# Kernel rows loaded as they lie and folded from channel-major columns, with a copy turned backwards, in a gated mix of two state-space layers

## The chip, the cores and the metric

One core of one Trainium2 chip runs the whole program. The metric is device time in microseconds (us), from the start of one execution to its end; less is better. In a profile the engines are called PE (TensorE matmuls; PEld is its weight load), DVE (VectorE), ACT (ScalarE), POOL (GpSimd) and SP (SyncE, which issues most transfers). Times inside a profile count from the start of its span.

## What is computed

The output is a gated sum of two layers over a sequence of S = 2048 positions and D = 1024 channels, all in bf16:

```python
g = sigmoid((x * gate_w).sum(-1, keepdims=True))
a = S5(x)      # complex diagonal recurrence over t, with B, C matrices of 1024 x 1024
b = H3(x, k, v)
return g * a + (1 - g) * b

# H3, for each channel d:
k_shift[t] = sum over i < 4 of k[t - i] * shift_k[i]
kv = k_shift * v
y = irfft(rfft(kv, 2S) * rfft(ssm_k, 2S))[:S]     # a causal convolution of length 2048
return x * (y + kv * ssm_D)
```

ssm_k holds one row of 2048 taps for each channel: shape (1024, 2048), the channel outermost.

## The kernel before

The H3 layer works through eight chunks of 128 channels (NC = 8). The sequence is cut into four blocks of 512 positions (TB), and the transform of a block is a matmul with tables of cosines and sines. As those are even and odd, a block of 512 is first folded: its upper 256 positions plus and minus its lower 256 mirrored about the middle. For the convolution kernel this fold is `fold_K(c)` (lines 471 to 484). It takes the tile kn, which holds positions on the partitions (128) and [16 blocks of 128 positions, 128 channels] beside them. Two matmuls of 512 columns for each of sum and difference and each half mt of the fold, one with the identity `ident` as weights and one with `refl` (the identity with its columns turned, with sign +1 or -1), build the sum in PSUM; a matmul with one row adds ssm_D at position 0. ACT copies the PSUM tile foldk to the tile eok. The last chunk uses `mirror_K` instead.

So kn must have positions on its partitions, while ssm_k lies in memory with the channel outermost: `load("kn", c)` (lines 184 to 191) issues a transposing transfer, `load_t`, on SP.

After the fold, `fwd_K` does the forward transform (PSUM tiles psk, copied by ACT to Kh or into BT); `taps` makes k_shift from kT, the transposed k; `times_v` multiplies by v, mirrors (PSUM tile mirror, ACT copy lo, DVE difference ev); `fwd_V` gives Vh; `products` are DVE's complex products into G; `inverse` gives psz and cv, which goes to memory. Parts of the S5 layer (`Bu`: PSUM tiles odd and even, ACT copies U) are put between.

The order on each engine is written out by hand: every instruction that goes through `put` is tied behind the one before it on its engine (lines 92 to 95), so that calls in the text stand on the engine in that order. Work is written as generators that `step` and `run` move on. PSUM has four tiles in rotation (`psum`, line 81): a new tile waits until ACT or DVE has read the tile that had its buffer before. The tag ld has three buffers for kT, kn, kB and v.

The start (lines 1025 to 1067) is written out too: taps for chunk 0 and DVE's products with v, tables SF, CF and NCF, `columns` (parameter columns), `state_params` (small DVE operations abv, thn, nthn, then th and so on), `inverse_cols` and `inverse_angles` (the rows for the inverse table), the fold of chunk 0, its transforms and products. Then the loop over c from 0 to 6 (lines 1079 to 1199) works at three chunks at a time: products of chunk c, forward transforms of n = c + 1, and fold, taps and v of nn = c + 2, and issues the loads of c + 3. In the loop, ACT's order around the fold of chunk nn is: copies cv, lo, cv, then `dgs(nn)`, then the four evictions of psk of chunk n, then the evictions of foldk.

The first transfers: SP issues the two halves of kT for chunk 0, then kn for chunk 0; ACT's queue takes the shift taps (skr), the first half of v (`load_v0(0)`, line 165), three rows of parameters (line 167), then after a table load the second half of v, ssm_D and gate_w. Transfers that use the hardware queues take one of eight completion semaphores in turn, and a transfer waits until the one before it on its semaphore has landed.

Of the kernel before, what the change touches and what calls it, by code (L numbers as in the profile page):

```python
# [9 lines left out]
ALU = mybir.AluOpType  # L10
ACT = mybir.ActivationFunctionType
BF16 = mybir.dt.bfloat16
# [8 lines left out]
def kernel(  # L21
# [38 lines left out]
    TB = 512  # L60
# [25 lines left out]
    def ps2(shape, name):  # L86
        return psum.tile(shape, F32, name=name, tag="ps")
# [9 lines left out]
    def mm(o, l, r, first, last):  # L97
        put("pe", nc.tensor.matmul, o, lhsT=l, rhs=r, start=first, stop=last)
# [9 lines left out]
    def ts(o, a, s1, s2, op0, op1=None):  # L108
        if op1 is None:
            put("dve", V.tensor_scalar, out=o, in0=a, scalar1=s1, scalar2=None, op0=op0)  # L110
        else:
            put("dve", V.tensor_scalar, out=o, in0=a, scalar1=s1, scalar2=s2, op0=op0, op1=op1)

    def copy(o, a):
        put("dve", V.tensor_copy, o, a)

    def act(o, i, **kw):
        put("act", nc.scalar.activation, out=o, in_=i, **kw)

    def load_t(o, i):  # L120
        put("sp", nc.sync.dma_start_transpose, out=o, in_=i)

    def move(o, i):
        put("sp", nc.sync.dma_start, out=o, in_=i)
# [36 lines left out]
    def load_v0(h):  # L161
        ns = slice(h * NT // 2, (h + 1) * NT // 2)
        nc.scalar.dma_start(out=v0[:, ns], in_=vf.rearrange("(n p) d -> p n d", p=128)[:, ns, 0:128])

    load_v0(0)
    for i, ap in enumerate((A_log_dt, A_Lambda_re, A_Lambda_im)):
        nc.scalar.dma_start(out=prow[i * ND:(i + 1) * ND, :], in_=ap.rearrange("(j p) -> j p", p=128))
    pih = consts.tile([128, 1], F32, name="pih")
    put("dve", nc.vector.memset, pih, math.pi / 2.0)
    magic = consts.tile([128, 1], F32, name="magic")  # L170
# [10 lines left out]
    def hold(column):  # L181
        act(column, pih, func=ACT.Copy)

    def load(which, c, held=False):
        cc = slice(c * 128, (c + 1) * 128)
        if which == "kn":

            t = ld.tile([128, NT, 128], BF16, name="kn", tag="ld")
            if held:
                hold(t[:, 0, 0:1])  # L190
            load_t(t, B_ssm_k[cc, :])
        elif which == "v":

            w = 2 if c == 2 else 1
            if c == NC - 1:
                t = ld.tile([128, NT, 128], BF16, name="v", tag="ld")
            elif c == 2:
                lds["v2"] = xt_pool.tile([128, NT, 2, 128], BF16, name="v2", tag="xT")
            if c < 2:
                t = ld.tile([128, NT, 128], BF16, name="v", tag="ld")  # L200
            elif c < NC - 1:
                t = lds["v2"][:, :, c % 2:c % 2 + w].rearrange("p n k d -> p n (k d)")
            if held:
                hold(t[:, 0, 0:1])
            move(t, vf.rearrange("(n p) d -> p n d", p=128)[:, :, c * 128:(c + w) * 128])
            for k in range(w):
                lds["v", c + k] = t[:, :, k * 128:(k + 1) * 128]
            return
        else:

            t = ld.tile([128, PAD + S], BF16, name="kT", tag="ld")
            put("pool", nc.gpsimd.memset, t[:, 0:PAD], 0.0)
            if held:
                hold(t[:, PAD:PAD + 1])
            load_t(t[:, PAD:], kf[:, cc])
            if c >= 3:
                lds["kB", c] = ld.tile([128, PAD + S], BF16, name="kB", tag="ld")
        lds[which, c] = t
# [35 lines left out]
    def iota_i32(shape, pattern, base, mult, name):  # L254
        ti = u4(shape, I32, name + "_i")
        nc.gpsimd.iota(ti, pattern=pattern, base=base, channel_multiplier=mult)
        return ti

    def iota_f32(shape, pattern, base, mult, name, home=None):
        ti = iota_i32(shape, pattern, base, mult, name)  # L260
        t = u4(shape, F32, name) if home is None else home.tile(shape, F32, name=name)
        copy(t, ti)
        return t

    def flat(ap):
        return ap.rearrange("p a b -> p (a b)")
# [20 lines left out]
    SI = tab_pool.tile([128, 2, 512], BF16, name="SI")  # L287
    colm_i = iota_i32([128, 2], [[256, 2]], 1, 2, "colm")
    fr_i = iota_i32([128, 512], [[4, 512]], 1, 0, "fr_")
    ident = consts.tile([128, 128], BF16, name="ident")  # L290
    make_identity(nc, ident)
    raised = ps2([128, 2, 512], "raised")

# [7 lines left out]
    nc.gpsimd.memset(refl, 0.0)  # L301
    for k, v in enumerate((1.0, -1.0)):
        nc.gpsimd.affine_select(out=refl[:, k], in_=refl[:, k], pattern=[[1, 128]], base=-127, channel_multiplier=1,
                                compare_op=ALU.not_equal, fill=v)
    colm = consts.tile([128, 2], F32, name="colm")
    ts(colm, colm_i, 1.0 / 4096.0, None, ALU.mult)
# [52 lines left out]
    inv = {}  # L359

    def inverse_cols():
        colf = iota_f32([128, 2], [[512, 2]], 1, 4, "colf", home=consts)
        inv["col"] = consts.tile([128, 2], F32, name="colneg")
        inv["at0"] = consts.tile([128, 2], F32, name="colat0")
        ts(inv["col"], colf, -1.0 / 2048.0, None, ALU.mult)
        ts(inv["at0"], colf, 511.0 / 2048.0, None, ALU.mult)

    def inverse_angles():

# [9 lines left out]
    def inverse_table():  # L379

        yield from sincos(flat(inv["room"]), 1024, flat(SI), flat(CI), -TWO_PI)
# [89 lines left out]
    def fold_K(c):  # L471

        kb = lds.pop(("kn", c)).rearrange("p (a f) d -> p a f d", f=4)
        eo = eos["k", c] = eo_pool.tile([128, 2, 2, 4, 128], BF16, name="eok")
        for mt in range(2):
            ps = ps2([128, 2, 4, 128], "foldk")
            for e in range(2):
                mm(ps[:, e], ident, kb[:, :, 2 + mt], True, False)
                mm(ps[:, e], refl[:, e], kb[:, :, 1 - mt], False, mt == 0)
                if mt == 1:  # L480

                    mm(ps[:, e, 0], refl[0:1, e], sD[:, c * 128:(c + 1) * 128], False, True)
            act(eo[:, :, mt], ps, func=ACT.Copy)
            yield

    def mirror_K(c):
# [131 lines left out]
    def fwd_V(c, fis=range(NFI)):  # L618
        eo = eos["v", c]
        if c not in VH:  # L620
            VH[c] = spectrum("V", c)
        for fi in fis:
            fsl = slice(fi * 128, (fi + 1) * 128)
            ps = ps2([128, 2, 4, 128], "psv")
            for cc in range(2):
                tab = CF if cc == 0 else SF
                for mt in range(2):
                    mm(ps[:, cc], tab[:, mt, fsl], eo[cc][:, mt], mt == 0, mt == 1)
            act(of_tile(VH[c], fi), ps, func=ACT.Copy, scale=2.0 / 1024.0)
# [384 lines left out]
    def step(gen):  # L1014
        next(gen, None)

    def run(gen):
        for _ in gen:
            pass
# [5 lines left out]
    none = iter(())  # L1025
    first = first_times_v(0, dg0)
    step(first)
    act(flat(SF), rqf, func=ACT.Sin, scale=TWO_PI)
    put("dve", V.scalar_tensor_tensor, out=flat(hf), in0=rqf, scalar=-1.0, in1=rqf, op0=ALU.mult, op1=ALU.max)
    act(flat(CF), flat(hf), func=ACT.Sin, bias=pih, scale=-TWO_PI)  # L1030
    columns = columns()
    step(columns)
    trow[0] = tab_pool.tile([128, TB], mybir.dt.float16, name="row")
    copy(trow[0], flat(iota_i32([128, 2, HB], [[1, 2], [2, HB]], 0, 0, "row")))
    sp = state_params()
    step(sp)
    step(first)
    inverse_cols()
    ts(NCF, CF, -1.0, None, ALU.mult)
    step(first)  # L1040
    angles = inverse_angles()
    turns = inverse_table()
    run(columns)
    run(fold_K(0))
    step(sp)
    step(angles)
    run(first)
    dg1 = dgs(1, True)
    run(angles)
# [2 lines left out]
    load("kn", 1)  # L1052
    fwd_K(0, (0, 1))
    fwd_V(0, (0, 1))
    step(turns)
    taps(1, dg1)
    step(sp)
# [21 lines left out]
    for c in range(NC - 1):  # L1079
# [47 lines left out]
        step(tabs)  # L1127
        run(back)
        run(old)
        if nn < NC:  # L1130
            dg = dgs(nn)
        if c == 2:
            step(parts)
        fwd_K(n, (0, 1))
# [6 lines left out]
            run(sp)  # L1141
            gate(0)
        step(prod)
        fk = none
        if nn < NC:
            fk = fold_K(nn) if c < 5 else mirror_K(nn)
            step(fk)
            if c < 5:
                step(fk)
            if c == 4:  # L1150
                step(parts)
            if c == 1:
                load_BT(1, 0, True)
            elif c < 5:
                load("v", nn, True)
            step(parts)
            taps(nn, dg)
            if c == 5:
                load("v", nn)
                load_xT(2, held=True)  # L1160
            if nn + 1 < NC:
                load("kT", nn + 1, True)
                load("kn", nn + 1)
                apart = spread(nn + 1)
                step(apart)
                if c == 1:
                    load_BT(1, 1)
                elif c in (2, 3):
                    load_xT(1, (3 - c,))
                run(apart)  # L1170
# [297 lines left out]
```

## Time and profile before

| what | us |
|---|---|
| median of 3 runs | 388.48 (388.27 to 388.70) |
| the profiled execution | 385.94 |
| its span, from first to last instruction | 384.2 |
| PE busy in the span | 373.1 |
| DVE busy in the span | 371.7 |
| ACT busy in the span | 294.3 |

The granted clock of TensorE was 0.999 of full speed. Busy times are of one profiled execution. A matmul of 512 columns is listed with some 380 ns, but such matmuls start 215 ns apart: they are pipelined, and the spacing of their starts, not their listed length, is what a row of them costs. The DMA engines are busy in nearly every slice of the span; 45.6 MB of the 70.7 MB moved go over the queue of SP and its transposing loads.

| stage | from | to |
|---|---|---|
| start, to the first product of chunk 0 on DVE | 0 | 19.4 |
| rest of chunk 0's products | 19.4 | 47.2 |
| chunk loop c = 1 to 5, five products of 23 to 24 us each | 47.2 | 164.8 |
| last chunks, then the S5 layer and the output | 164.8 | 384.2 |

### The profile page before, as it was taken

The numbers are of one execution on the slowest core, as the hardware profiler recorded it, in microseconds if no ns is written. First come the engines' busy times: TensorE is split into PE (matmuls) and PEld (weight loads), VectorE is DVE, ScalarE is ACT, GpSimd is POOL, SyncE is SP. The second block draws the span as 40 slices with busy tenths as digits, with TensorE's granted clock in tenths as the row PEclk, the third lists the DMA queues.
The fourth block names the chain that finished last, engine by engine and source line by source line (L and its number), as shares of the span: only waits on it lengthen the run. The fifth ranks groups of instructions, "written<-read, shape, count | busy, mean of one in ns | idle before, by whom it ended". The sixth has DMA issues, their size and how long they took to land.

```text
span 384.2 us, 6583 instructions
## 1 busy us (share of the span) xinstructions
PE 373.1 (97%) x2411; PEld 196.2 (51%) x2445; DVE 371.7 (97%) x602; ACT 294.3 (77%) x448; POOL 77.1 (20%) x101
## 2 busy tenths in 40 slices
PE   7999899999999999999999999999999999999995
PEld 4556347565484756754454444444444444444442
DVE  8899999999999999999999999999999999999996
ACT  5799997988979789774678799775988869937601
POOL 3011030110301102030002300413414323635000
PEclk9999999999999999999999999999999999999999
DMA  8969999999999997957696999896899999898903
GB/s 166 166 131 226 183 221 213 224 202 146 230 201 221 212 189 162 198 136 136 115 208 142 204 258 203 199 196 122 157 224 184 222 247 236 139 258 153 225 2 109
DMA packets 135506, 70.72 MB, mean 184 GB/s; under 512 B 114921, under 2 KB 117745, under 8 KB 135474
## 3 DMA queue, kind: packets, MB, share of 16 engines
q1 hardware_dynamic: 120912, 45.64, 55.4%
q0 software_dynamic: 12400, 24.12, 36.8%
q10 hardware_dynamic: 2162, 0.54, 0.8%
q8 instruction: 19, 0.31, 0.3%
q14 instruction: 13, 0.11, 0.1%
HBM read 12.86 MB, written 8.39 MB: 55 GB/s over the span
## 4 chain that ended last, share of the span: by engine, by line
PE 75%; DVE 14%; ACT 4%; issue 3%; DMA 3%; SPq 1%; DVEq 0%
PE psy L94 29%; PE both L94 17%; PE psk L94 7%; DVE BT L94 5%; PE psz L94 5%; PE taps L94 4%; DVE wkh L94 4%; PE even L94 3%; PE psv L94 3%; PE foldk L94 3%; PE odd L94 3%; DVE G L94 2%; ACT Vh L94 1%; DMA BT<-in_A_B_im_dram 1%; DMA kT<-in_B_k_dram 1%
## 5 line engine op out<-in xcount | busy, mean ns | idle before, releaser
L94 PEld LDWEIGHTS <-BT 128*128 128x128 bf16 x640 | 61.7, 98 | 49.0 <-DMA BT<-in_A_B_im_dram 0.9
L94 PE MATMUL both<-xT,BT 128*128 128x512 bf16 x375 | 83.4, 379 | 0.9 <-DMA BT<-in_A_B_im_dram 0.4
L94 POOL DMA_DIRECT2D U<-Q x22 | 23.3, 1071 | 90.2 <-ACT Q L94 55.3
L94 PEld LDWEIGHTS <-hb 128*128 128x128 bf16 x256 | 24.9, 98 | 30.2 <-issue 0.3
L94 PEld LDWEIGHTS <-U 128*128 128x128 bf16 x240 | 23.5, 98 | 28.3
L94 PE MATMUL psy<-CT,hb 128*128 128x512 bf16 x156 | 36.6, 379 | 0.2
L94 ACT ACTIVATE Vh<-psv 128x1024 bf16<-128x1024 f32 x32 | 30.8, 1033 | 7.7 <-PE psv L94 7.6
L94 ACT ACTIVATE U<-both 128x512 bf16<-128x512 f32 x44 | 24.2, 594 | 16.0 <-PE both L94 15.5
L94 PE MATMUL psy<-CT,U 128*128 128x512 bf16 x149 | 34.3, 379 | 0.1
L94 DVE TENSOR_TENSOR_SCAN W<-rv,init,A 128x256 bf16<-128x256 f32 x48 | 32.2, 732 | 0.0
L94 POOL DMA_DIRECT2D G<-wkh x8 | 9.7, 1218 | 101.7 <-DVE wkh L94 101.7
L94 ACT ACTIVATE Q<-U,lam 128x512 bf16<-128x512 bf16 (+1 forms) x44 | 25.4, 607 | 3.9 <-DMA CT<-Q 3.9
L94 PE MATMUL psk<-eok,SF 128*128 128x512 bf16 (+1 forms) x119 | 27.9, 354 | 0.3
L94 PEld LDWEIGHTS <-SF 128*128 128x128 bf16 x184 | 18.0, 98 | 19.6 <-issue 1.1
L94 PE MATMUL psz<-G,CI 128*128 128x512 bf16 x64 | 24.3, 380 | 1.4 <-DVE G L94 1.3
L94 PE MATMUL psz<-G,SI 128*128 128x512 bf16 x64 | 24.3, 379 | 0.0
L94 PE MATMUL psy<-CTa,hb 128*128 128x512 bf16 x95 | 22.6, 379 | 0.1
L94 PE MATMUL taps<-dg,kT 128*128 128x128 bf16 (+1 forms) x352 | 21.3, 207 | 1.3 <-DMA kT<-in_B_k_dram 1.3
L94 PEld LDWEIGHTS <-kT 128*128 128x128 bf16 x352 | 20.6, 98 | 2.8 <-DMA kT<-in_B_k_dram 2.2
L94 DVE TENSOR_TENSOR wkh<-BT,Vh 128x3072 bf16<-128x3072 bf16 (+4 forms) x20 | 21.8, 1112 | 0.0
L94 DVE TENSOR_TENSOR wkh<-Kh,Vh 128x3072 bf16<-128x3072 bf16 (+2 forms) x16 | 21.3, 1351 | 0.0
L94 PE MATMUL psy<-CTa,U 128*128 128x512 bf16 x87 | 20.4, 379 | 0.1
(221 smaller groups left out, 838.9 us busy)
## 6 DMA issues: line engine op xcount, KB each, us to landing
U<-Q POOLq DMA_DIRECT2D x22, 256.0 KB, 5.1
G<-wkh POOLq DMA_DIRECT2D x6, 768.0 KB, 8.3
cv_scr<-cv SPq DMA_DIRECT2D x16, 256.0 KB, 3.8
v<-in_B_v_dram SPq DMA_DIRECT2D x5, 512.0 KB, 5.8
out_dram<-m SPq DMA_DIRECT2D x8, 256.0 KB, 6.3
BT<-cv_scr SPq DMA_DIRECT2D x7, 256.0 KB, 7.1
out_dram<-BT SPq DMA_DIRECT2D x7, 256.0 KB, 3.8
ks<-lo POOLq DMA_DIRECT2D x6, 256.0 KB, 7.7
```

What stands on the lines that cost most here:

```text
L94: i = f(*a, **kw)
```

## The change

For chunks 0, 3, 4, 5 and 6 (`by_channel`) kn is loaded with a plain transfer, a channel's row of 4096 bytes to one partition. The new `fold_columns` folds it: first a copy `back` (tile lo) takes the lower 256 positions of each block in reverse order, on DVE for chunk 0 and on ACT for the others; then, for each half mt and each of the four blocks, 128 columns of kn serve as weights against [identity, identity] and 128 columns of back as weights against [identity, -identity], 256 columns each, so that the transposition happens on PE and sum and difference come out side by side. The evictions of foldk to eok are as many and as large as before, with the axes of the PSUM tile in another order.

The reversed copy is put in the loop behind `dgs(nn)` and ahead of the evictions of psk; the matmuls stay where the fold was. For chunk 0 the copy stands on DVE ahead of the first product with v.

Around it: the first half of v is issued behind the three parameter rows on ACT's queue, which also gives it and them other completion semaphores, and kn of chunk 0 shares one with the first parameter row instead of v. The casts of row and colf and its two scalings go from DVE to ACT, ahead of SF; the angle rows come ahead of the fold's evictions on ACT; `state_params` begins after the fold, so that its table load on ACT and its first three DVE operations come later. POOL makes two more 128x128 identities, one of them negative.

```diff
-    load_v0(0)
     for i, ap in enumerate((A_log_dt, A_Lambda_re, A_Lambda_im)):
         nc.scalar.dma_start(out=prow[i * ND:(i + 1) * ND, :], in_=ap.rearrange("(j p) -> j p", p=128))
+    load_v0(0)
...
+    def by_channel(c):
+        return c == 0 or 3 <= c < NC - 1
...
         if which == "kn":
-            t = ld.tile([128, NT, 128], BF16, name="kn", tag="ld")
-            if held:
-                hold(t[:, 0, 0:1])
-            load_t(t, B_ssm_k[cc, :])
+            if by_channel(c):
+                t = ld.tile([128, S], BF16, name="kn", tag="ld")
+                move(t, B_ssm_k[cc, :])
+            else:
+                t = ld.tile([128, NT, 128], BF16, name="kn", tag="ld")
+                load_t(t, B_ssm_k[cc, :])
...
-    ident = consts.tile([128, 128], BF16, name="ident")
+    idents = consts.tile([128, 3, 128], BF16, name="ident")
+    ident = idents[:, 0]
...
+    nc.gpsimd.memset(idents[:, 1:], 0.0)
+    for k, v in ((1, 1.0), (2, -1.0)):
+        nc.gpsimd.affine_select(out=idents[:, k], in_=idents[:, k], pattern=[[1, 128]], base=0, channel_multiplier=-1,
                                 compare_op=ALU.not_equal, fill=v)
...
     def inverse_cols():
-        colf = iota_f32([128, 2], [[512, 2]], 1, 4, "colf", home=consts)
+        colf = iota_i32([128, 2], [[512, 2]], 1, 4, "colf")
         inv["col"] = consts.tile([128, 2], F32, name="colneg")
         inv["at0"] = consts.tile([128, 2], F32, name="colat0")
-        ts(inv["col"], colf, -1.0 / 2048.0, None, ALU.mult)
-        ts(inv["at0"], colf, 511.0 / 2048.0, None, ALU.mult)
+        act(inv["col"], colf, func=ACT.Copy, scale=-1.0 / 2048.0)
+        act(inv["at0"], colf, func=ACT.Copy, scale=511.0 / 2048.0)
...
+    def fold_columns(c):
+        kn = lds.pop(("kn", c)).rearrange("p (a t) -> p a t", t=TB)
+        back = eo_pool.tile([128, 4, 2, 128], BF16, name="lo", bufs=2)
+        rev = back.rearrange("p a f d -> p a (f d)"), kn[:, :, 255::-1]
+        if c == 0:
+            copy(*rev)
+        else:
+            act(*rev, func=ACT.Copy)
+        yield
+        eo = eos["k", c] = eo_pool.tile([128, 2, 2, 4, 128], BF16, name="eok")
+        for mt in range(2):
+            ps = ps2([128, 4, 2, 128], "foldk")
+            for a in range(4):
+                withD = mt == 1 and a == 0
+                mm(ps[:, a], kn[:, a, 256 + mt * 128:384 + mt * 128], idents[:, 0:2], True, False)
+                mm(ps[:, a], back[:, a, mt], idents[:, 1:3], False, not withD)
+                for e in range(2 if withD else 0):
+                    mm(ps[:, a, e], refl[0:1, e], sD[:, c * 128:(c + 1) * 128], False, e == 1)
+            act(eo[:, :, mt], ps.rearrange("p a e d -> p e a d"), func=ACT.Copy)
+            yield
...
     step(first)
+    trow[0] = tab_pool.tile([128, TB], mybir.dt.float16, name="row")
+    act(trow[0], flat(iota_i32([128, 2, HB], [[1, 2], [2, HB]], 0, 0, "row")), func=ACT.Copy)
+    inverse_cols()
     act(flat(SF), rqf, func=ACT.Sin, scale=TWO_PI)
...
     step(columns)
-    trow[0] = tab_pool.tile([128, TB], mybir.dt.float16, name="row")
-    copy(trow[0], flat(iota_i32([128, 2, HB], [[1, 2], [2, HB]], 0, 0, "row")))
-    sp = state_params()
-    step(sp)
+    fk = fold_columns(0)
+    step(fk)
     step(first)
-    inverse_cols()
     ts(NCF, CF, -1.0, None, ALU.mult)
     step(first)
     angles = inverse_angles()
     turns = inverse_table()
+    step(angles)
     run(columns)
-    run(fold_K(0))
+    run(fk)
+    sp = state_params()
     step(sp)
-    step(angles)
     run(first)
...
     fwd_V(0, (0, 1))
+    step(sp)
     step(turns)
...
+        fk = none
         if nn < NC:
             dg = dgs(nn)
+            if by_channel(nn):
+                fk = fold_columns(nn)
+                step(fk)
...
-        fk = none
         if nn < NC:
-            fk = fold_K(nn) if c < 5 else mirror_K(nn)
+            if not by_channel(nn):
+                fk = mirror_K(nn)
             step(fk)
```

## The prediction, made before the changed kernel was run

> **What bounds the kernel now.** I read the page first, then the chain of waits in order of time, then the timeline of the start, the DMA packets of the start by stretch, and last DVE, ACT and PE beside each other in the chunk loop. The page's busy line:
>
> ```profile
> PE 373.1 (97%) x2411; PEld 196.2 (51%) x2445; DVE 371.7 (97%) x602; ACT 294.3 (77%) x448; POOL 77.1 (20%) x101
> ```
>
> Two engines are full at once, so a gain must shorten both, or fall where one of them stands idle. The chain of waits (start, length, what) says where that is:
>
> ```profile
> 0.75 4.90 DMA kT<-in_B_k_dram
> 5.69 1.96 PE taps L94 x32
> ...
> 10.10 2.27 PE foldk L94 x10
> ...
> 12.39 1.03 ACT eok L94
> ...
> 56.36 2.15 PE foldk L94 x10
> ```
>
> The start hangs on a transfer, then on PE and ACT through the fold of chunk 0; from 46 to 137 us the chain runs almost wholly on PE. The timeline of the start:
>
> ```profile
> 0.75 2.59 SPq L94 DMA_TRANSPOSE kT<-in_B_k_dram  x2
> 1.34 0.43 ACTq L163 DMA_DIRECT2D v<-in_B_v_dram  x1
> 5.54 2.09 SPq L94 DMA_TRANSPOSE kn<-in_B_ssm_k_dram  x1
> 6.01 1.22 DVE L94 SCALAR_TENSOR_TENSOR h<-rq 128x1024 f32<-128x1024 f32 x1
> 9.71 0.42 DVE L94 TENSOR_SCALAR NCF<-CF 128x1024 bf16<-128x1024 bf16 x1
> 12.93 1.22 DVE L94 TENSOR_TENSOR ev<-ks,mirror 128x1024 bf16<-128x1024 bf16 x1 [1.03 <-PE foldk L94]
> 19.36 1.23 DVE L94 TENSOR_TENSOR G<-BT,Vh 128x2048 bf16<-128x2048 bf16 x1 [0.75 <-ACT Vh L94]
> ```
>
> kn is issued 2.2 us after SP is free (3.34): in the built program it waits for v's first load, with which it shares a completion semaphore, and 1.34 plus that load's 4.2 us to landing is 5.54. The DMA packets in the stretch 3.25 to 4.5 us (q10 is ACT's queue, q1 SP's):
>
> ```profile
> q10 hardware_dynamic: 1046, 0.26, 112.3%
> q1 hardware_dynamic: 130, 0.03, 16.2%
> ```
>
> The stretch before has 933 packets of q1 alone, the one after 1040 of q1. So v's first half (256 KB, 1024 packets) runs between the two halves of kT, and kT's first half, moved by about 3.5, lands only at 5.65. In the loop, DVE's first product of three chunks waits for Vh:
>
> ```profile
> 94.54 2.29 DVE L94 TENSOR_TENSOR G<-Kh,Vh 128x4096 bf16<-128x4096 bf16 x1 [0.21 <-ACT Vh L94]
> 117.82 2.29 DVE L94 TENSOR_TENSOR G<-BT,Vh 128x4096 bf16<-128x4096 bf16 x1 [0.17 <-ACT Vh L94]
> 141.28 2.29 DVE L94 TENSOR_TENSOR G<-Kh,Vh 128x4096 bf16<-128x4096 bf16 x1 [0.36 <-ACT Vh L94]
> ```
>
> These 0.74 us are all that DVE can win there. ACT and PE in the chunk c = 3:
>
> ```profile
> 100.33 1.09 ACT L94 ACTIVATE dg<-ident,pcol 128x64 bf16<-128x64 bf16 x4
> 101.28 3.79 ACT L94 ACTIVATE BT<-psk 128x1024 bf16<-128x1024 f32 x4
> ...
> 103.23 0.38 PE L94 MATMUL foldk<-kn,ident 128*128 128x512 bf16 x1
> ...
> 105.48 1.92 PE L94 MATMUL odd<-xT,BT 128*128 128x256 bf16 x16
> ```
>
> **The start, step by step.** v's first load moves behind three parameter loads on ACT's queue (0.50, 0.32 and 0.58 us): issued at about 2.8 instead of 1.34. kT's halves then follow each other undisturbed. The transposed kn, alone on the engines, was complete 0.3 to 0.5 us after its last packets (until 9.25 to 9.5, landed 9.74); kT's first half, last packets at 3.5, lands so at 4.0, or with the 1.2 us of a v load still in between at 5.2; I take 4.6, and taps begins 1.1 us earlier. PE then needs, as before, 10.10 - 5.69 = 4.4 us to the fold: 9.0. Fold 2.05 (below), eviction 1.05, then 5.9 from there to Vh (13.42 to 19.33 before): 18.0 instead of 19.33.
>
> DVE does not start earlier: its table arithmetic ends at 7.23 in both. From there: pcol 0.1; the new reversed copy, L; product 1.22; NCF 0.36; product 1.22; three small copies 0.3; PE's mirror 0.25; then 5.7 to G's start as before (12.93 to 18.61, its own readiness) and 0.45 for abv, thn and nthn, which move from before ev to here. That is 16.8 + L for G. Gone from DVE: the row cast (0.42), colf and its two scalings (0.34). ACT takes these (0.6 and 0.3) before SF, which slips from 6.0 to about 6.4; NCF, the first reader of CF on DVE, comes over 1 us later, so nothing. POOL's new memset (0.6) and two selects (0.36 each) push the row iota from 3.29 to 4.6, inside the same cover. ACT's table load (1.28) and dtv move from 8.43 to behind eok, where ACT before did rv and the two angle rows (1.7): 0.1 at most, since the first psk needs PE 1.2 us anyway.
>
> L is unknown: nearest rows are NCF, the same shape forwards (0.42), and the PSUM product of 1024 (1.22). I take 0.6, nearer the former because the types and places are its own. The new wait: the copy needs kn, and DVE's two products, ev and through mirror PE stand behind it. kn, now waiting only for the first parameter row, is issued at about 3.4, needs SP about 0.5 (v's plain loads) instead of 2.09, and carries 0.52 MB, which the transposed load moved in 2.3 us. The engines are taken by kT until 4.8 and by v's two halves for 1.25 us each. kn lands between 7.4 (ahead of v) and 9.7 (behind both); I take 8.2. G starts at 8.2 + 9.5 + 0.6 = 18.3, against PE's 18.0: 1.0 us gained. Ends: 16.8 + 0.42 gives way to PE's 18.0 (1.3 gained); 9.7 + 9.5 + 1.22 = 20.4 (1.0 lost).
>
> The Trainium skill, VectorE: DVE Perf Modes, What auto-detection actually checks, lets a 16-bit copy keep its fast mode at a step of +1 or -1. By that rule L is 0.42 and G starts at 18.1; no run here shows a negative step.
>
> **The loop, chunks 3 to 6.** PE: a fold took 105.48 - 103.23 = 2.25 us: eight matmuls of 512 columns 0.215 apart, and two one-row matmuls that cost 0.25 each. Now 16 of 256 columns: odd, 16 pairs of weights and 256 columns, goes from 105.48 to 107.23, 1.75 us. The one-row pair stands together: 0.3. So 2.05, 0.2 less, four times: 0.8 gained. Below: 0 if the one-row pair costs 0.5.
>
> ACT: one more pass of 128x1024 bf16 per chunk, behind dg and ahead of the psk evictions; row: eok<-kn, 1.06 us, the next starting 0.94 later. Behind it stand four evictions that free PSUM for PE. c = 1: the first is then over at 54.9, the fold that takes its buffer starts at 56.2: covered by 1.3. c = 2: 79.5 against psk at 80.06: covered by 0.5. c = 3: 101.28 + 0.94 + 1.02 = 103.24 against 103.23: 0.1 with the semaphore. c = 4: 126.54 against even at 126.51: 0.1. ACT then catches up in its idle 1.49 us before Vh. If the reversed pass is longer, every tenth over 0.94 costs PE twice, over 1.5 three times.
>
> Plain loads save SP about 2 us a chunk and 0.5 to 1 us of the DMA engines; kn is read a chunk later (issued 67.73, read at 77.5), so that is worth nothing, and costs nothing while loads stay a chunk ahead. PE gains 0.8 - 0.2 = 0.6; DVE could take 0.74. I take 0.5. Past 141 DVE sets the end up to 189.8, and the rest follows it: nothing else changes.
>
> **Sum.** 1.0 + 0.5 - 0.1 = 1.4 us. The profiled execution took 385.94 (span 384.2 and 1.7 around it) and would take 384.5. The median of the runs shown, 388.48, is 2.5 above that execution; with the same difference: 387.1. What a measurement of this kernel can tell from no change is about 0.2%, 0.8 us.
>
> **Rivals.** (1) kn lands behind v's second half, near 9.3: DVE waits for it, G starts at 19.4, the start gains nothing and 0.5 - 0.1 stays: 388.1. For it: both v halves are issued before kn, and the trace shows whole loads running one after the other. Against: they stand on another queue, and kT's two halves ran on either side of one. Chance 0.2.
> (2) Slower: the reversed read is slow on ACT, a place in the loop without cover. Where the next pass starts 2.0 us later instead of 0.94, PE waits 0.5, 1.1 and 1.1 in c = 2, 3, 4; less 0.8 of the folds that is 1.9 late, less 0.9 at the start: 388.5 + 1.0 = 389.5. It decides from about 1.9 on. No row has a reversed operand; the forward ones are all near 1.06. Chance 0.12.
> (3) The twofold number of weight loads shows. Eight more at the 98 ns of a LDWEIGHTS row make a fold 2.05 + 0.8 = 2.85 us, 0.6 over 2.25; four are 2.4 late, and with 0.2 of ACT and 0.9 gained at the start that is 388.5 + 1.7 = 390.2. Against it stand odd's 16 pairs in 1.75 us, weights included. Chance 0.03.
> The Trainium skill, TensorE: Matmul & The Clock Gate, The mechanism, says that weight loads overlap running matmuls only in other row groups, which would make (3) true; odd's pairs, all of full height, disagree.
> (4) The change does what it says but kT lands no earlier, since v's load was not in its way: start 0.3, loop 0.5, less 0.1: 387.8; it is in (1)'s neighbourhood, chance 0.05, faster or same by a hair.
>
> The forecast has 0.6, its own range 386.4 to 387.7. Faster: 0.6 and a little of (4), 0.62. Same: 0.22. Slower: (2), (3) and the late, slow copy of the start, 0.16. The range leaves out (3), half of (2) and a gain over 2.5: 386.0 to 389.3.
>
> **What would show it.** Right: kT's wait ending near 4.6, kn issued near 3.4, G at 18.0 to 18.6, folds of 2.05 us, the three Vh waits nearly gone, ACT's lo<-kn near 1.06. Wrong: DVE idle in front of its lo<-kn until past 9; lo<-kn near 1.2 on DVE or 2 on ACT; PE waiting for psk evictions in c = 3 and 4; fold matmuls more than 0.12 apart.

## The result and the profile after

The changed kernel took 386.12 us (median of 16 runs), the kernel before 388.06 (16 runs, 385.85 to 389.05); the ratio is 0.9955, 95% interval 0.994 to 0.9969, so 1.2 to 2.3 us less. Forecast were 387.1 and a range of 386.0 to 389.3: sign and size hold, though the time lies only 0.1 above the lower bound and below the narrower range, 386.4 to 387.7, to which the forecast gave 0.6. The way to them does not hold, as the profile shows.

One execution of the changed kernel among the 16 was disturbed (2238 us) and is left out of the ratio; the profile after is therefore that of the first experiment, the same kernel run again (384.5 us span, 386.24 with what lies around it). Its busy line, to be set beside the one of before:

```profile
PE 373.7 (97%) x2451; PEld 201.0 (52%) x2485; DVE 371.5 (97%) x599; ACT 298.3 (78%) x455; POOL 77.3 (20%) x104
```

Nothing got shorter here, and the span is 0.3 us **longer** than that of the kernel before (384.2). The chain of waits, start and one fold of the loop (start, length, what):

```profile
5.75 4.57 DMA rows<-in_gate_w_dram
10.32 0.05 issue
10.37 0.51 PE p L94 x8
10.88 2.26 PE foldk L94 x18
...
13.16 1.03 ACT eok L94
```

Before, the start hung on kT until 5.65 and then on PE. Now it hangs on the gate's row, a load of 2 KB that the prediction did not count, and kT is off the chain. The timeline of the start (SP's and ACT's issues, PE, DVE):

```profile
0.74 2.60 SPq L94 DMA_TRANSPOSE kT<-in_B_k_dram  x2
2.66 0.44 ACTq L163 DMA_DIRECT2D v<-in_B_v_dram  x1
3.84 0.37 SPq L94 DMA_DIRECT2D kn<-in_B_ssm_k_dram  x1
4.34 3.14 PE L94 MATMUL taps<-dg,kT 128*128 128x128 bf16 x32
7.94 1.96 PE L94 MATMUL taps<-dg,kT 128*128 128x128 bf16 x32 [0.34 <-DMA kT<-in_B_k_dram]
10.14 0.43 DVE L94 COPY lo<-kn 128x1024 bf16<-128x1024 bf16 x1 [2.28 <-DMA kn<-in_B_ssm_k_dram]
20.75 1.17 DVE L94 TENSOR_TENSOR G<-BT,Vh 128x2048 bf16<-128x2048 bf16 x1
```

taps starts at 4.34 instead of 5.69 and without a wait; then 32 matmuls take 3.14 us, where before they took 1.96. DVE waits for kn until 10.14, and G starts at 20.75, 1.4 us later than in the profile before. Why kn is so late stands in the DMA packets of the stretch 6 to 7 us, when it has been under way for over 2 us (q10 is ACT's queue with v, q1 SP's with kn):

```profile
q10 hardware_dynamic: 875, 0.22, 134.0%
q1 hardware_dynamic: 32, 0.00, 2.4%
```

In the loop, PE's fold and DVE's first products:

```profile
103.96 0.27 PE L94 MATMUL foldk<-ident,kn 128*128 128x256 bf16 x1
...
106.02 1.91 PE L94 MATMUL odd<-xT,BT 128*128 128x256 bf16 x16
```

```profile
95.00 2.28 DVE L94 TENSOR_TENSOR G<-Kh,Vh 128x4096 bf16<-128x4096 bf16 x1
...
118.33 2.29 DVE L94 TENSOR_TENSOR G<-BT,Vh 128x4096 bf16<-128x4096 bf16 x1 [0.23 <-ACT Vh L94]
...
141.69 2.29 DVE L94 TENSOR_TENSOR G<-Kh,Vh 128x4096 bf16<-128x4096 bf16 x1 [0.26 <-ACT Vh L94]
```

A fold takes 106.02 - 103.96 = 2.06 us (2.25 before). Of the three waits for Vh one is gone, two stay (0.23 and 0.26, before 0.17 and 0.36).

How can a kernel whose profile is 0.3 us longer be 1.7 us faster by the medians of the first experiment? Because the profile before is not of the usual run. The first set of runs beside the experiments has 35 of the kernel before: nine from 385.7 to 386.1 and 26 from 387.1 to 388.8, with nothing between; with the two later sets it is 14 of 84 up to 386.45, with a median of 385.8, and 70 from 387.03 to 389.19, with a median of 387.9. The profile before (385.94) is of the small group. The changed kernel's 12 runs beside them lie in one group, 385.34 to 386.35. So what the change does is to take away the large group.

### The profile page after: what moved, and what is told of

Read it like the earlier page. It is cut to its first block, busy times and chain, and to the rows that moved or that the text cites. A ratio compares the mean times of both kernels' runs of the same rounds, so it can differ in the third digit from the quotient of the medians.

```text
span 2236.4 us, 6704 instructions
## 1 busy us (share of the span) xinstructions
PE 2231.0 (100%) x2485; PEld 696.5 (31%) x2485; DVE 374.3 (17%) x599; ACT 310.1 (14%) x455; POOL 76.5 (3%) x104
## 4 chain that ended last, share of the span: by engine, by line
PE 100%; DVE 0%; DVEq 0%; issue 0%
PE psy L94 30%; PE both L94 23%; PE psk L94 13%; PE psv L94 8%; PE psz L94 8%; PE taps L94 5%; PE even L94 5%; PE odd L94 4%; PE foldk L94 4%; PE mirror L94 1%; PE p L94 1%; PE raised L94 0%; DVE BT L94 0%; DVEq L1502 0%; DVE wkh L94 0%
## 5 line engine op out<-in xcount | busy, mean ns | idle before, releaser
L94 PE MATMUL both<-xT,BT 128*128 128x512 bf16 x384 | 508.8, 1705 | 0.0
L94 PEld LDWEIGHTS <-BT 128*128 128x128 bf16 x640 | 204.1, 320 | 464.3 <-issue 464.1
L94 PE MATMUL psy<-CT,hb 128*128 128x512 bf16 x160 | 216.8, 1704 | 0.0
L94 PE MATMUL psy<-CT,U 128*128 128x512 bf16 x152 | 205.2, 1707 | 0.0
L94 PE MATMUL psk<-eok,SF 128*128 128x512 bf16 (+1 forms) x120 | 152.3, 1555 | 0.0
L94 PE MATMUL psy<-CTa,hb 128*128 128x512 bf16 x96 | 131.1, 1701 | 0.0
L94 PE MATMUL psy<-CTa,U 128*128 128x512 bf16 x88 | 119.6, 1708 | 0.0
L94 PE MATMUL psv<-ks,SF 128*128 128x512 bf16 x64 | 96.8, 1703 | 0.0
L94 PE MATMUL psv<-ev,CF 128*128 128x512 bf16 x64 | 96.7, 1704 | 0.0
L94 PE MATMUL psk<-eok,CF 128*128 128x512 bf16 x64 | 96.6, 1708 | 0.0
```

What stands on the lines that cost most here:

```text
L94: i = f(*a, **kw)
```

## The experiments

Each was timed beside the kernel before, in three sets: the first four kernels (median of before 387.49), the next four (388.06), the last four (387.78). Where a difference to the changed kernel is given across sets, it is the difference of the two differences to before. "Clock" stands for the speed of PE: the program begins with matmuls without use (`raise_clock`, tile raised) that keep PE busy so that it speeds up. The table holds each profiled execution's start times of DVE instructions, as the difference to the first profile before (first row), and the time at which the trace's clock record of PE first says full speed:

| kernel | median | clock up | G | ev, chunk 1 | G, c = 3 | G, c = 4 | G, c = 5 | last G | span |
|---|---|---|---|---|---|---|---|---|---|
| before, first profile | | 4.28 | 19.36 | 29.49 | 94.54 | 117.82 | 141.28 | 189.80 | 384.2 |
| before, second profile | | 9.08 | +1.57 | +1.56 | +1.59 | +1.56 | +1.59 | +1.58 | 385.8 |
| changed | 385.75 | 6.86 | +1.39 | +0.76 | +0.46 | +0.51 | +0.41 | +0.39 | 384.5 |
| start only | 386.42 | 5.67 | +1.22 | +0.60 | +0.60 | +0.56 | +0.58 | +0.57 | 384.9 |
| loop only | 386.87 | 8.85 | +1.42 | +1.42 | +1.12 | +1.16 | +1.06 | +1.05 | 385.1 |
| v ahead again | 387.17 | 9.32 | +2.10 | +1.48 | +1.17 | +1.21 | +1.11 | +1.10 | 385.2 |
| before, PE kept busy | 386.29 | 7.17 | +0.61 | +0.61 | +0.61 | +0.58 | +0.61 | +0.61 | 384.8 |
| gate behind the fold | 385.63 | 4.88 | +0.61 | -0.02 | -0.30 | -0.26 | -0.36 | -0.36 | 384.2 |
| v's move alone | 386.65 | 8.61 | +1.05 | +1.06 | +1.05 | +1.02 | +1.05 | +1.04 | 385.2 |
| changed, with a gap | 385.99 | 9.32 | +1.38 | +0.76 | +0.47 | +0.51 | +0.41 | +0.40 | 384.5 |
| v behind the table load | 386.38 | 7.59 | +1.31 | +0.70 | +0.39 | +0.44 | +0.33 | +0.34 | 384.4 |
| v behind row | 385.47 | 5.83 | +0.55 | -0.07 | -0.37 | -0.33 | -0.43 | -0.43 | 383.6 |
| v's second half behind row | 386.24 | 6.25 | +1.32 | +0.69 | +0.40 | +0.45 | +0.34 | +0.35 | 384.4 |

The column "ev, chunk 1" reads what the start is worth, the step from there to "G, c = 5" what the loop is worth.

### The changed kernel again, and its two halves

> The changed kernel as it is, for a profile that can be set beside that of the kernel before. Theory (start 0.9 us, loop 0.5 us): 1.4 to 2 us under the kernel before; kT's wait ends near 4.6 instead of 5.65, G starts at 18.0 to 18.6 instead of 19.36, folds of chunks 3 to 6 take 2.05 us instead of 2.25. Rival A (all of it is the start): G starts at 17.6 or sooner and the loop gains under 0.2. Rival B (all of it is the loop): G starts at 19 or later and the stretch from G's start to 141 us is over 1.2 us shorter.

Measured: 385.75 us (12 runs), ratio 0.9964 (0.9944 to 0.9983), 1.7 us under before. kT and the folds (2.06) as expected. G at 20.75 is against the theory and rival A; rival B had it at 19 or later, but its stretch from there to 141 us is 0.98 us shorter (141.28 - 19.36 before, 141.69 - 20.75 here), not over 1.2. The loop gave 0.35 (0.76 to 0.41).

Start only: chunk 0 alone is folded the new way.

```diff
     def by_channel(c):
-        return c == 0 or 3 <= c < NC - 1
+        return c == 0
```

> The changed kernel with only chunk 0 folded from channel-major columns; chunks 3 to 6 load kn transposed and fold it as in the kernel before. Theory: 0.9 us under the kernel before, so 0.5 to 1 us over the changed kernel. Rival A (all of it is the start): equal to the changed kernel within 0.3 us. Rival B (all of it is the loop): equal to the kernel before within 0.3 us.

Measured: 386.42 (386.22 to 386.78, one group), by medians 1.1 under before and 0.7 over the changed kernel, as the theory has it; the ratio, 0.9985 (0.9968 to 1.0002), doesn't resolve it from no change. But its start is later than that of the first profile before (+0.60), so the 1.1 is no earlier start against that profile.

Loop only: the kernel before with `fold_columns` for chunks 3 to 6 and nothing of the new start.

```diff
+    def by_channel(c):
+        return 3 <= c < NC - 1
```

> The kernel before with only the folds of chunks 3 to 6 changed: plain loads, ACT's copy turned backwards, 16 matmuls of 256 columns; start and v's first load as before. Theory: 0.5 us under the kernel before. Rival A (start alone): equal to the kernel before within 0.3 us, or up to 0.3 over it. Rival B (loop alone): 1.4 to 2 us under it.

Measured: 386.87, ratio 0.9994 (0.9975 to 1.0014), again in two groups (385.26 to 385.86; 386.69 to 388.16): 0.6 by medians, not resolved by the interval. Its profile shows the loop's worth without the scatter of the start: +1.42 to +1.06, 0.36 us, the same as in the changed kernel. By medians the two halves add up: 1.07 and 0.62, 1.74 for both; neither half alone is resolved by its interval.

### v's first load put back

```diff
+    load_v0(0)
     for i, ap in enumerate((A_log_dt, A_Lambda_re, A_Lambda_im)):
         nc.scalar.dma_start(...)
-    load_v0(0)
```

> The changed kernel with v's first load put back ahead of the three parameter rows. Theory (kT's halves held apart by v, and kn held back by v's completion): kT's wait ends near 5.65 again, kn is issued near 5.5 and lands near 8.5 to 9; G starts at 18.9 to 19.5; 0.7 to 1.1 us over the changed kernel. Rival (v's place does not matter, the plain load and the shorter work on DVE do): within 0.3 us of the changed kernel.

Measured: 387.17 (385.34 to 387.77), ratio 0.9994 (0.9975 to 1.0014): 1.4 over the changed kernel, and one run at 385.34 apart from eleven at 386.75 and over. The whole gain of the start hangs on this line, plain load or not. kT's wait ends at 5.58 and kn is issued at 5.39, as expected, but G starts at 21.46, 2 us past the expectation. The line in PE's timeline is what led on:

```profile
5.58 3.60 PE L94 MATMUL taps<-dg,kT 128*128 128x128 bf16 x32 [1.22 <-DMA kT<-in_B_k_dram]
```

Same start as in the first profile before (5.69 after a wait of 1.33), but 3.60 instead of 1.96 us: in the trace the single matmuls start 107 ns apart instead of 56. PE ran at half speed.

### Is it PE's clock? The kernel before once more, and with PE kept busy

> The kernel before, unchanged, for a second profile. The 35 runs of it beside the first four experiments lie in two groups, 385.7 to 386.1 (nine) and 387.1 to 388.8 (26). Theory (PE's clock): the first profile was of the first group, whose first 32 matmuls of taps are 56 ns apart. In a run of the second group they are 107 ns apart, their group takes 3.5 us instead of 1.96, full speed is recorded from 8.4 us or later instead of 4.28, and G starts 1.4 to 3 us later, at 20.8 to 22.4. Rival (transfers): taps keeps its 56 ns in a run of the second group too, and kT or kn lands over 1 us later than in the first profile.

Measured: 387.56, of the large group. PE's timeline:

```profile
5.63 3.59 PE L94 MATMUL taps<-dg,kT 128*128 128x128 bf16 x32 [1.26 <-DMA kT<-in_B_k_dram]
```

kT lands where it did; the matmuls are 107 ns apart; the clock record says full speed from 9.08; G starts 1.57 us later, and every later row of the table is later by the same amount. kn is issued at 5.58 and takes its 4.2 us, as before, but now the fold waits for PE until 11.60. The theory of the clock holds for this run, the rival of the transfers falls.

Then the remedy that touches nothing but the clock, in the kernel before:

```diff
         ts(dg0[:, k], ident, pcol[:, 3 + k, 0:1], None, ALU.mult)
-    raise_clock(3)
+    raise_clock(6)
```

> The kernel before with six instead of three clock-raising matmuls ahead of taps, so that PE does not idle between 4.34 us and kT's landing. Theory (PE's clock rises at the end of the first window of about 3.4 us in which PE was busy, wherever that window falls in the run): the rise falls anywhere from 4.3 to 7.8 us, taps loses 0 to 1.5 us; one broad group of 385.8 to 387.4, median 386.3 to 386.9, and none above 387.6; the median over 0.5 us under the kernel before. Rival (the two groups come from transfers): two groups as in the kernel before, medians within 0.3 us of each other.

Measured: 386.29, ten of 11 runs from 385.76 to 386.56 and one at 387.76 (0.2 over the bound set); ratio 0.9958 (0.9943 to 0.9973). Its profile:

```profile
3.73 1.91 PE L94 MATMUL raised<-wkh 128*128 128x512 bf16 x4
5.54 2.73 PE L94 MATMUL taps<-dg,kT 128*128 128x128 bf16 x32
```

PE has no gap, and its speed doubles within taps, at 7.17. Three matmuls without use bring the kernel before as much as the whole change (0.9958 against 0.9955 and 0.9964): the large group is shown to come from PE's idle 1.3 us ahead of taps. What the one run at 387.76 is was not found.

### v's move alone, and the changed kernel with a gap

The kernel before with only v's first load behind the parameter rows:

> The kernel before with one line of the change: v's first load behind the three parameter rows; kn transposed and all folds as before. Theory (the gain is that kT's first half lands as PE's clock-raising matmuls end, so that PE has no idle 1.3 us there and its clock rises by 7.8 us in every run): taps starts at 4.3 to 4.6, one group of runs with none above 387.2, median 385.9 to 386.6, so 1 us or more under the kernel before without any new fold. Rival (the plain load and the new fold of chunk 0 are what gains at the start): within 0.4 us of the kernel before, two groups of runs again.

Measured: 386.65 (eleven runs from 386.18 to 387.69, one at 390.0), ratio 0.9986 (0.9967 to 1.0005), 1.1 under before by medians, not resolved by the interval. Half right: the gain of 1 us came, but not one group with none above 387.2. taps waits until 5.10, not 4.3 to 4.6: the transposing kn, now issued at 3.66, probably goes between kT's packets, as the plain kn with its 128 packets of 4 KB does not. The gap on PE is 0.74 us and the clock in this profile came up only at 8.61, but taps starts 0.5 us earlier than in the second profile before, and that stays to the end (+1.04 against +1.58).

The changed kernel without the clock-raising matmuls ahead of taps:

```diff
-    raise_clock(3)
```

> The changed kernel without the second group of three clock-raising matmuls, so that PE idles from 2.9 us to kT's landing at 4.3 to 4.6. Theory (PE's clock): the rise falls between 7.4 and 11.5 us instead of 4.3 to 7.8, the first 32 taps run 107 ns apart in most runs and in some the second 32 and the fold too; the start waits for kn and the gate's row until 10.3, so only rises later than 8 us cost: the median 0.3 to 1.2 us over the changed kernel and the spread of the runs 1.5 us or more instead of 1.0. Rival (the clock has no part in the changed kernel's time): within 0.15 us of the changed kernel, and no wider.

Measured: 385.99 (385.68 to 386.73), 1.8 under before, as the changed kernel itself is (1.7). The theory's number was wrong here, the rival's right. The profile says how:

```profile
4.21 3.60 PE L94 MATMUL taps<-dg,kT 128*128 128x128 bf16 x32 [1.24 <-DMA kT<-in_B_k_dram]
...
7.87 2.63 PE L94 MATMUL taps<-dg,kT 128*128 128x128 bf16 x32
```

The clock came up at 9.32, all of the first and half of the second group ran at half speed, and PE was through at 10.43. What the fold needs was there by then:

```profile
9.52 0.43 DVE L94 COPY lo<-kn 128x1024 bf16<-128x1024 bf16 x1 [1.37 <-DMA kn<-in_B_ssm_k_dram]
10.43 0.51 PE L94 MATMUL p<-ident,rows 8*128 8x8 bf16 x9
10.87 0.28 PE L94 MATMUL foldk<-ident,kn 128*128 128x256 bf16 x1
```

kn was in at 9.52, nothing waits for the gate's row, and the chain of this execution runs from kT through PE to the fold. So here the slow clock sets the start of the fold, 10.87; in the changed kernel's profile late transfers set it, 10.81. The two limits lie side by side, and that is luck. So the changed kernel is not kept safe by a busy PE. It bears a slow clock because taps starts 1.4 us earlier (4.21, in the second profile before 5.63), which leaves PE no later than the transfers of the changed kernel's profile.

### What binds the new start

The gate's transposes put behind the fold:

```diff
-    run(columns)
-    run(fk)
+    run(fk)
+    run(columns)
```

> The changed kernel with the gate's transposes and the other small matmuls of the second part of columns put behind the fold of chunk 0 on PE, transfers as they are. Theory (the gate's row at 10.3 and kn at 10.1 bind together): the fold starts at 10.15 to 10.3 on kn and waits for the copy until 10.6, its second matmul onwards; eok's end comes 0.2 to 0.4 us earlier and the time falls by 0.2 to 0.4. Rival (the gate's row alone binds): 0.6 us or more. Rival (kn alone binds): within 0.1 us of the changed kernel.

Measured: 385.63 (6 runs, 385.32 to 386.31), 2.4 under before against 1.7: 0.7 better where 0.2 to 0.4 were expected, but the intervals overlap (0.993 to 0.9958, and 0.9944 to 0.9983). The profile gains 0.78 at the start, and not all of it by the new order: kn was there at 9.36, 0.78 sooner than in the changed kernel's profile, with the transfers in the same order. The fold's second matmul, the first that needs the copy, started at 9.85; 0.78 later is 10.63, against 10.93 in the changed kernel. So the order is worth some 0.3 by this estimate, and the rest is kn's. kn's landing scatters from run to run; that the changed kernel's time scatters with it is likely, not shown.

Both halves of v behind the table load were meant to put kn ahead of v:

```diff
+    nc.scalar.dma_start(out=sD, ...)
+    nc.scalar.dma_start(out=gwr, ...)
-    load_v0(0)
     ...
+    load_v0(0)
     load_v0(1)
...
```

> The changed kernel with the two small rows (D and the gate's) ahead of v on ACT's queue and both halves of v behind ACT's first table load, so that kT's second half and kn go ahead of v. Theory (the start of the changed kernel is bound by transfers: kn at 10.1 and the gate's row at 10.3 come behind v): kn lands near 8, the fold starts at 9.7 to 10.1 instead of 10.9, G at 19.6 to 20.2 instead of 20.75; 0.5 to 1 us under the changed kernel, so 384.8 to 385.3. Rival (the sum of the bytes binds, not their order): v's halves land near 10 to 11, DVE's two products of taps and v come later by what the copy gains, and the time stays within 0.3 us of the changed kernel.

Measured: 386.38 (385.49 to 388.18), ratio 0.9969 (0.9952 to 0.9986). It did not do what it was made for: kn now shares its completion semaphore with the third small load, waits for it until 4.57, and v is issued at 3.61, so kn still landed at 10.06.

With v written behind ACT's cast of row, kn has no wait and is issued at 3.56, v at 4.39 and 4.84 (in the built program still ahead of that cast, which runs at 5.47, but behind kn):

```diff
     act(trow[0], flat(iota_i32(...)), func=ACT.Copy)
+    load_v0(0)
+    load_v0(1)
```

> The changed kernel with the two small rows ahead of v, and both halves of v issued behind ACT's cast of row (near 5.6 us), which in the built program also leaves kn without a wait (issued at 3.4). Experiment with v behind the table load had kn issued at 4.57, still behind v at 3.61, so it did not test this. Theory (kn and the gate's row bind the changed kernel's start because they come behind v): kn lands at 7 to 8, the fold starts on PE's own time, 9.3 to 10.2, instead of 10.9, v's second half lands at 10 to 10.5, G starts at 19.5 to 20.2; 0.4 to 1.2 us under the changed kernel. Rival (the bytes bind, not their order): the products of taps and v wait for v until 10 and 11, mirror and ev come no sooner than 13.8, within 0.2 us of the changed kernel.

Measured: 385.47, all six runs from 385.41 to 385.50; ratio 0.9944 (0.9927 to 0.9961). DVE's timeline:

```profile
8.50 0.43 DVE L94 COPY lo<-kn 128x1024 bf16<-128x1024 bf16 x1 [0.64 <-DMA kn<-in_B_ssm_k_dram]
9.62 1.23 DVE L94 TENSOR_TENSOR ks<-taps,v 128x1024 bf16<-128x1024 f32 x1 [0.70 <-DMA v<-in_B_v_dram]
...
19.91 1.17 DVE L94 TENSOR_TENSOR G<-BT,Vh 128x2048 bf16<-128x2048 bf16 x1
```

kn is there at 8.5, the fold starts at 9.41 instead of 10.81, the wait moves to v's first half, and G starts 0.84 us earlier than in the changed kernel: the order of the transfers binds, not their sum. This is the best profile of all (383.6) and the steadiest; that it beats the changed kernel in measured time (2.3 under before against 1.7) is likely but not settled, since the intervals overlap.

Last, only v's second half behind the cast of row:

> As the kernel with v behind the cast of row, but only v's second half there; the first half stays behind the rows, so that the order of the transfers is kT, v's first half, kn, v's second half. Theory: kn lands at 8.5 to 9.2 and the first product is not delayed: fold at 9.5 to 10.3, 0.4 to 1 us under the changed kernel. Rival (the bytes bind): within 0.2 us of it.

Measured: 386.24, in two groups (seven runs at 385.96 to 386.29, five at 387.48 to 387.82). Here too kn got a wait on a small load and was issued at 4.48, behind both halves of v (3.55 and 4.06), so the order that was wanted did not come about; it landed at 10.07 in the profile, which is of the lower group. What the upper group is was not found. The mean granted clock on record for each run tells it apart: 0.993 to 0.996 in the five, 0.998 to 1.000 in the seven. The five slowest runs with v behind the table load (386.98 to 388.18) have 0.993 to 0.996 too, the seven others 0.997 to 1.000. No profile is of such a run.

## Why the prediction was right, and where it was not

**The base line was wrong, and made the rest come out.** The prediction saw that the median lay 2.5 us above the profiled execution and carried this over as a constant. It was the sign of two groups of runs, and the profile was of the rarer one. The start of 19.36, from which 1.0 us was to be gained, is a start with a fast clock; in the usual run it is 20.9 (second profile). That the sum of the terms met the measured time is luck.

**kT.** Forecast 4.6; taps starts at 4.15 to 4.60 in the profiles of the changed kernel and its variants with v behind: right. Rival 4 falls with it. It was worth more than thought: taps starts without PE's long gap, and where a slow clock is forced, PE is still through by 10.43.

**kn, the term that failed.** Issued at 3.84 (forecast 3.4), landed at 10.14 in the changed kernel's profile, and at 9.96, 9.36 and 9.52 in three variants with the same order of transfers (forecast 8.2, bounds 7.4 and 9.7). Rival 1 describes what happened, v's two halves ahead of kn; its price (no gain at the start, 388.1) was reckoned from the wrong base. With kn ahead of v, 8.5.

**The gate's row was missing.** It is issued at 5.75 behind a load of D that held ACT's queue for 1.92 us (0.43 before), lands at 10.32, and eight small matmuls ahead of the fold need it. A 2 KB load ended the chain.

```profile
3.79 1.92 ACTq L176 DMA_DIRECT2D rows<-in_B_ssm_D_dram  x1
```

**The reversed copy.** 0.43 us on DVE, the row of NCF; 0.6 was taken. The Trainium skill, VectorE: DVE Perf Modes, What auto-detection actually checks, lets a copy of 16-bit values keep its fast mode at a step of -1, from which the prediction had estimated 0.42: this trace agrees. On ACT 1.05 to 1.08, as the forward rows: rival 2 falls.

**The fold.** 2.06 in the loop against 2.05: right, with the matmuls 109 ns apart, weight loads included, so rival 3 falls. In chunk 0, where 2.05 was forecast too, it gave nothing: from its first matmul to eok's start 13.16 - 10.81 = 2.35, before 12.39 - 10.03 = 2.36.

**The loop.** Forecast 0.5, found 0.35 and 0.36. PE gained 0.18 to 0.19 in each of the four folds, and lost 0.09 at the psk evictions in c = 4, as reckoned (0.1). But PE then came to wait for DVE: its first psz of c = 3 starts 0.06 us after the end of DVE's product G<-BT in both profiles (91.59 + 2.36 = 93.95 and 94.01; before 90.84 + 2.36 = 93.20 and 93.26), and here that gave back 0.35, all that PE had won by then. The rows, first of before, then of the changed kernel:

```profile
90.84 2.36 DVE L94 TENSOR_TENSOR G<-BT 128x2048 bf16<-128x2048 bf16 x2
92.55 1.96 ACT L94 ACTIVATE Vh<-psv 128x1024 bf16<-128x1024 f32 x2
93.26 0.39 PE L94 MATMUL psz<-G,CI 128*128 128x512 bf16 x1
...
91.59 2.36 DVE L94 TENSOR_TENSOR G<-BT 128x2048 bf16<-128x2048 bf16 x2
94.01 0.39 PE L94 MATMUL psz<-G,CI 128*128 128x512 bf16 x1 [0.37 <-ACT Vh L94]
```

The profile puts the wait down to ACT's Vh, but before, psz started at 93.26, ahead of the end of the first of those two passes (92.55 and some 1.0), so it doesn't need them. DVE won 0.30 where its first wait for Vh went; the second and third stayed (0.23 and 0.26 against 0.17 and 0.36). "The three Vh waits nearly gone" was the step that failed: a gain of PE counts only as far as DVE can follow.

**Moves said to cost nothing.** rv now stands behind Vh on ACT (19.97, before 13.31), and DVE waits 0.82 us for it in front of G; the 0.63 between "G" and "ev, chunk 1" is this delay, made good by that ev. POOL's new operations made DVE's product end at 7.76 instead of 7.23, in front of a wait for kn until 10.14.

**Net.** Against the first profile before, with its fast clock, the changed kernel's profile loses 0.76 at the start and wins 0.35: 0.4 slower. Against the second it wins 1.56 - 0.76 = 0.8 and 0.35, and the two executions are 387.56 - 386.24 = 1.3 us apart. The rest of the measured 1.7 is that this profile of the changed kernel lies 0.5 above the median of its set (385.75); against before's small group, with a median of 385.8, the medians show no gain. That the slower runs of before's large group have a still later clock is argued, not shown, since no profile is of one. The mean granted clock on record for each run fits it: in all thirteen profiles the record of full speed is 375.47 or 378.88 us long, and half speed follows, so a mean of 1.000 means that its end came late. In the large group of the first set, the seven runs up to 387.32 have 0.998, the nine from 387.42 to 387.82 0.999, and nine of the ten from 387.91 on 1.000.

## What to carry to other kernels

Look at the single times before the median: if they fall in two groups, find out which one the profile is of, since a sum made on the rarer group sets its terms against the wrong path. A short PE idle right after its first matmuls (1.3 us here) can cost more than the idle itself (G 1.57 later), and some matmuls without use in the gap can be worth a whole change. When a load is moved, follow every load behind it on all queues, the smallest too, and which completion semaphore each then shares.

## What the runs showed of the hardware

PE's speed doubles at a moment that differs from run to run. Where PE had no gap over 0.3 us between its first matmul (1.19) and that moment, full speed was recorded between 4.88 and 7.59; with a gap of 0.7 to 1.3 us it came at 8.61 to 9.32, save for the first profile before, where it was up at 4.28, ahead of the gap, and stayed up through it. The column of the granted clock says 1.00 all the while (in the changed kernel's profile for each of four stretches between 1.19 and 9.9); the spacing of the matmuls (107 or 56 ns) tells the truth. The Trainium skill, TensorE: Matmul & The Clock Gate, Part 1: The HAM clock gate, says that the clock rises after about 3.4 us of sustained work, judged in a window that runs free of the program, so that the same kernel differs from run to run. These runs agree: the rise comes 3.1 to 8.1 us after the first matmul, and the two lengths of the record of full speed, 375.47 and 378.88 us, are 3.41 apart.

POOL slows DVE: beside POOL's selects and iota, DVE's four dg operations took 0.92 instead of 0.81 us and the first rq operation 1.10 instead of 0.68, in all nine profiles with POOL's new operations and in none of the four without:

```profile
3.65 0.54 POOL L313 TENSOR_SCALAR_AFFINE_SELECT ident<-ident 128x128 bf16<-128x128 bf16 x2
4.14 0.56 POOL L261 IOTA row_i<- 128x512 int32 x1
...
4.15 1.10 DVE L94 TENSOR_SCALAR rq<-h 128x1024 f32<-128x1024 f32 x1
```
